# The last batch of attention with its 320-query steps first, in a fused attention and two-product kernel

## The chip, the cores and the metric

One NeuronCore of a Trainium2 chip. The metric is the time of one execution on the device, in microseconds (us). Engines: PE is TensorE (matmuls), PEld its weight loads, DVE VectorE, ACT ScalarE, POOL GpSimd, SP SyncE, which here issues the DMAs.

## The reference

```python
# q, k, v: 4 batches x 8 heads x 576 x 64; s: 4 x 8 x 576
scores = q @ k.T / sqrt(64)                       # per batch and head
cum = cumsum(max(s, 0))
scores = where(causal, -1e9, scores + minimum(-(cum[:, None] - cum[None, :]), 0))
attn = exp(scores - max(scores)); attn /= sum(attn) + 1e-9
x = (attn @ v), heads side by side                # 2304 x 512
h = x @ w_in                                      # 2304 x 2048
x2 = (h * cos(h)) @ w_out                         # 2304 x 512
out = maximum(maximum(x2 @ w1, x2 @ w2), x2 @ w3) @ wo2     # 2304 x 768, then x 512
```

## The kernel before

Nearly every product is made of halves: an operand is split into a high and a low 16-bit part, and three matmuls (high x high, high x low, low x high) stand for one.

**Attention** goes in 32 steps (`STEPS`), a step being one batch b, one query range r and one pair p of heads. Range 0 is queries 0 to 255 (two units of 128 queries), range 1 queries 256 to 575 (units 2, 3, and unit 4 with 64 queries of both heads). A range-0 step sees keys up to 256, a range-1 step all 576. Order before: batch, then range 0, 1, then the four pairs. Steps 20 to 23 are batch 2, range 1; steps 24 to 27 are batch 3, range 0; steps 28 to 31 are batch 3, range 1.

A step does, for each unit: scores on PE (L693, L697), masking and row minimum on DVE (L706), exp on ACT (L712), division and split into halves on ACT (L387) and DVE (L417), and a DMA transpose on SP's queue (L729) into one of two buffers `pt`. Score slots in PSUM, `e` and `pp` have two buffers each. Then the step's values (L759, attention times v) are gathered in one PSUM bank, bank 4, and evacuated as two halves by ACT (L772) and DVE (L777) into `x_b[r][p]`. There is one such buffer for each range and pair, and all batches use it in turn.

**v** of the next batch is loaded (five parts of up to 128 keys), its scale is found, and `v_split` splits each part into a ring of eight buffers. For batches 1 to 3, parts 0 and 1 are split after the last step of the batch before, and parts 2 to 4 ahead of the second step of the batch. Range 0 needs parts 0 and 1, range 1 all five.

**The first product**, h = x w_in, is `mm1(t)`, L906: one block of 16 chunks for each batch and range (`BLOCKS`, t = 2b + r, 0 to 7), each chunk two groups of six matmuls. The first group reads x of pairs 0 and 1, the second of pairs 2 and 3. It is placed behind the last pair of a range, ACT evacuates (L877) from three PSUM banks in turn, and h goes to DRAM.

**The gate and the second product.** Tiles of h come back from DRAM, h cos h is made with ACT's Sin (L1142), which has to wait for the last exp of attention (another table), and L1158 multiplies by w_out. Their scale needs all of w_out converted (L434 to L489, L950, L476). **The last stage** is L1242 and L1205.

**The order of the instructions** is not the program order above. `Plan` collects all operations with an engine, a planned duration, a key, and what they read and write; a write waits for the earlier readers and writers of its bytes. Then it walks through time and gives each engine the ready operation with the lowest key. Attention has keys of about 3 times the step's number, L906 has 1000 and up, L1158 2000 and up, the weight conversions 200 to 600. So attention goes first wherever it is ready, and L906 fills. Each engine then runs its list strictly in that order.

Of the kernel before, what the change touches and what calls it, by code (L numbers as in the profile page):

```python
# [23 lines left out]
B, H, S, D = 4, 8, 576, 64  # L24
# [4 lines left out]
NPAIR = H // 2  # L29
# [6 lines left out]

RANGES = ((0, 256, (0, 1)), (256, 320, (2, 3, 4)))
LAST = 4
STEPS = [(b, r, p) for b in range(B) for r in range(2) for p in range(NPAIR)]
BLOCKS = [(b, r) for b in range(B) for r in range(2)]  # L40
TB = 384
NTB = NT // TB
# [270 lines left out]
def attn_moe_kernel(ctx, tc, qT, kT, v, s, w_in, w_out, w1, w2, w3, wo2, out):  # L313
# [64 lines left out]
    def take(name, ring):  # L378
        n = rings.get(name, 0)
        rings[name] = n + 1  # L380
        return ring[n % len(ring)]
# [63 lines left out]
    def two(buf, cols):  # L445

        return (buf.ap(F16, cols), buf.ap(F16, cols, 2 * cols),
                [buf.span(0, 2 * cols)], [buf.span(2 * cols, 2 * cols)])

    def bound(value, sp, junk, junk_sp, col, col_sp, key, cols=512):  # L450

        P.add("ACT", act(cols, 0.28), key, lambda: nc.scalar.activation(
            out=junk, in_=value, func=AF.Abs, accum_out=col), reads=[sp], writes=junk_sp + [col_sp])

    def weight_load(src, cols, raw, key):
        m = load(raw.ap(I64, cols), src, 1024 * cols, key, writes=[raw.span(0, 8 * cols)])
        P.after(m, [rows_out])
        return raw.ap(I64, cols).bitcast(I32).rearrange("p (n two) -> p n two", two=2)
# [125 lines left out]
    def load_q(st, key):  # L584
        b, r, p = STEPS[st]
        q0, n = ((0, 256), (256, 384))[r]
        hb, lb = take("q", q_ring)
        hs, ls = [hb.span(0, 4 * n)], [lb.span(0, 4 * n)]
        raw = lb.ap(F32, n)
        load(raw, qT[b, p, :, q0:q0 + n], 512 * n, key - LEAD, writes=ls)  # L590
        if b == 0:
            q_of[st] = (raw, None, ls)
            return
        hi, lo = hb.ap(F32R, n), lb.ap(F32R, n)
        scaled(hi, raw, 1.0, key, n, ls, hs, on=Q_ON)
        minus(lo, raw, r_(hi), key + 0.2, n, ls + hs, ls, on=QS_ON)
        q_of[st] = (hi, lo, hs + ls)

    def load_k(b, p, key):
        hb, lb, rb = take("k", k_ring)  # L600
        hs, ls, rs = ([z.span()] for z in (hb, lb, rb))
        raw = lb.ap(F32, S)
        load(raw, kT[b, p], 295e3, key - LEAD, writes=ls, issue=0.65)
        if b == 0 and p == 0:
            row = rb.ap(F32, S)
            for c0, c1 in ((0, 320), (320, S)):
                first_row(c0, c1, row, [rb.span(4 * c0, 4 * (c1 - c0))], -30 if c0 == 0 else F2_KEY)
            ones = one_b.ap(F32, 128)
            bias = [(ones[64 * h:64 * h + 64], row[64 * h:64 * h + 64]) for h in range(2)]
            bias.append((onef_b.ap(F32, 128), row))  # L610
            rs = [rb.span(), one_b.span(), onef_b.span()]
        else:
            row, ones = rb.ap(F32R, S), oner_b.ap(F32R, 128)
            gb = take("got", got_b)
            got, gs = gb.ap(F32, S), [gb.span()]
            for h in range(2):
                load(got[64 * h:64 * h + 2], rows_dram[b * H + 2 * p + h], 4608, key - LEAD,
                     reads=[dspan("rows"), dspan("rows", 1)], writes=gs)
            scaled(row, got, 1.0, key, S, gs, rs, on=K_ON)
            bias = [(ones[64 * h:64 * h + 64], row[64 * h:64 * h + 64]) for h in range(2)]  # L620
            bias.append((onec_b.ap(F32R, 128), row))
            rs = [rb.span(), oner_b.span(), onec_b.span()]
        if b == 0:
            k_of[b, p] = (raw, None, bias, ls + rs)
            return
        hi, lo = hb.ap(F32R, S), lb.ap(F32R, S)
        scaled(hi, raw, 1.0, key, S, ls, hs, on=K_ON)
        minus(lo, raw, r_(hi), key, S, ls + hs, ls, on=KS_ON)
        k_of[b, p] = (hi, lo, bias, hs + ls + rs)
# [9 lines left out]
    def attention(st):  # L639
        b, r, p = STEPS[st]  # L640
        q0, nq, units = RANGES[r]
# [163 lines left out]
    def v_max(b, key):  # L805
        ab, vb = am_b[b % 2], vs_b[b]
        am, vs = ab.ap(F32, 8), vb.ap(F32, 4)
        if b == 0:
            for j in range(5):
                v_load(b, j, key)  # L810
            P.add("DVE", dve1(2560), key, lambda: nc.vector.tensor_reduce(
                out=am[:, 5:6], in_=early_v.ap(F32, 2560), op=ALU.max, axis=AX.X,
                apply_absolute_value=True), reads=[early_v.span()], writes=[ab.span()])
        else:
            for j in range(5):
                t, rb = v_load(b, j, key)
                P.add("DVE", dve1(512), key, lambda j=j, t=t: nc.vector.tensor_reduce(
                    out=am[:, j:j + 1], in_=t, op=ALU.max, axis=AX.X, apply_absolute_value=True),
                    reads=[rb.span()], writes=[ab.span()])
            P.add("DVE", 0.08, key, lambda: nc.vector.tensor_reduce(  # L820
                out=am[:, 5:6], in_=am[:, 0:5], op=ALU.max, axis=AX.X),
                reads=[ab.span()], writes=[ab.span()])
        A = [ab.span()]
        P.add("DVE", dve2(128) + 0.06, key, lambda: nc.vector.tensor_scalar(
            out=dia_b.ap(F32, 128), in0=eye_b.ap(F32, 128), scalar1=am[:, 5:6], scalar2=None,
            op0=ALU.mult), reads=A + [eye_b.span()], writes=[dia_b.span()])
# [36 lines left out]
    def v_split(b, j, key):  # L863
        t, rb = v_load(b, j, key)
        vs = vs_b[b].ap(F32, 4)
        vb = take("v", v_b)
        vv = vb.ap(F16, 1024).rearrange("p (a c) -> p a c", a=2)
        split(vv[:, 0], vv[:, 1], t, vs[:, 1:2], key, 512, [rb.span()], [vs_b[b].span()],
              [vb.span(0, 1024)], [vb.span(1024)], j in V_POOL[b > 0], V_ON)
        v_of[b, j] = (vv, vb)  # L870
# [130 lines left out]
    staged = []  # L1001
    for st in range(len(STEPS)):
        b, r, p = STEPS[st]
        if st + 1 < len(STEPS):
            load_q(st + 1, 3 * st + Q0)
        if r == 0 and p == 1 and b > 0:
            for j in (2, 3, 4):
                v_split(b, j, 3 * st + 1)
        attention(st)
        if r == 1 and b + 1 < B:  # L1010
            load_k(b + 1, p, 3 * st + (6 if p else 3))
            if p == 0:
                v_max(b + 1, 3 * st + 1)
            if p == 1:
                v_scale(b + 1, 3 * st + 1)
            if p == 3:
                for j in range(2):
                    v_split(b + 1, j, 3 * st + 1)
        if st in WI_AT:
            i_ = WI_AT.index(st)  # L1020
            for c in range(NC1 * i_ // len(WI_AT), NC1 * (i_ + 1) // len(WI_AT)):
                rb = take("rw", raw_all)
                key = WI_KEY0 + WI_KEY * c
                words = weight_load(w_in[c], 512, rb, key - 4)
                value, sp = value_of(words, 512, rb.span(), wo_b[c], key)
                small = wg_b[c // G]
                hi, lo, his, los = two(wi_b[c], 512)
                bound(value, sp, hi, his, small.ap(F32, 8)[:, c % G:c % G + 1], small.span(), key)
                staged.append((value, sp, hi, lo, his, los))
                if c % G < G - 1:  # L1030
                    continue
                power(G, small, small, key, POW_BANK)
                h_scale(0, c // G, key)
                by = small.ap(F32, 8)[:, 7:8]
                for i, (value, sp, hi, lo, his, los) in enumerate(staged):
                    split(hi, lo, value, by, key, 512, [sp], [small.span()], his, los,
                          i in WI_POOL, "ACT")
                staged.clear()
        if st == WI_AT[-1]:
            mm1(0)  # L1040
            for g in range(NC1 // G):
                h_scale(1, g, 3 * st + 1)
            out_weights()
        if st == WO_MAX:
            largest_in()
        if p == NPAIR - 1 and st >= NPAIR:
            mm1(2 * b + r)
# [336 lines left out]
```

## Time and profile before

| | |
|---|---|
| median of 3 runs | 868.19 us (866.1 to 868.93) |
| the profiled execution | 869.63 us, span 867.9 us |
| PE busy | 825.9 us, 95% of the span |
| DVE busy | 618.7 us, 71% |
| ACT busy | 536.8 us, 62% |
| mean granted clock of PE | 0.984 |
| DMA, hardware queue | 52.7% of 16 engines' span |

Times inside the span count from its start. Attention ends with the values of step 31 at 366.92 us, the first product at 395.4 us, the second product at 582.5 us; the rest is the last stage. "Busy" is the sum of the durations of an engine's instructions without overlaps. The granted clock is 1.00 at 2.4 GHz and 0.50 at 1.2 GHz.

### The profile page before, as it was taken

What the parts mean: (1) busy time and instruction counts of PE and PEld (TensorE: products, weight loads), DVE (VectorE), ACT (ScalarE), POOL (GpSimd) and SP (SyncE); (2) the same over time, 40 slices, a digit from 0 to 9 for tenths busy, and PEclk for the clock granted to TensorE, in tenths of its full rate; (3) what the DMA queues carried; (4) which work ended last, traced back from release to release, by engine and by line L of the source; (5) the groups of instructions that cost most, each with busy time, mean ns of one, the idle gap of its engine ahead of it and who ended that gap; (6) DMA issues with size and microseconds to landing.
All of it is one profiled execution on the core that took longest, in us unless ns stands there. A gap on an engine that the chain in (4) does not pass through costs nothing.

```text
span 867.9 us, 16606 instructions
## 1 busy us (share of the span) xinstructions
PE 825.9 (95%) x6078; PEld 522.7 (60%) x6078; DVE 618.7 (71%) x1593; ACT 536.8 (62%) x1209; POOL 55.6 (6%) x86
## 2 busy tenths in 40 slices
PE   6887789998999899999999999999999999999998
PEld 3556656786678667878544444446655555555564
DVE  7999998986999789866899999999523213322220
ACT  3778878986887778598999999824112113211211
POOL 4501321111010100000000000000000000000000
PEclk9889989999999989999999999999999999999999
DMA  8789988999999999854354443341000000000001
GB/s 246 172 209 224 263 204 193 242 227 234 245 206 244 222 226 236 223 163 137 108 153 140 135 156 110 112 129 40 1 16 21 13 25 25 1 25 13 37 1 48
DMA packets 156541, 117.70 MB, mean 136 GB/s; under 512 B 109902, under 2 KB 132686, under 8 KB 156460
## 3 DMA queue, kind: packets, MB, share of 16 engines
q1 hardware_dynamic: 156460, 116.65, 52.7%
q8 instruction: 47, 0.77, 0.4%
q14 instruction: 34, 0.28, 0.1%
HBM read 66.67 MB, written 23.74 MB: 104 GB/s over the span
## 4 chain that ended last, share of the span: by engine, by line
PE 64%; DVE 11%; DMA 4%; issue 2%; ACT 1%; POOL 0%; SPq 0%; ACTq 0%; DVEq 0%; POOLq 0%
PE banks L1242 24%; PE banks L1158 22%; PE banks L1205 8%; PE banks L906 7%; DMA p<-p 4%; DVE p L417 3%; DVE p L706 2%; PE banks L759 1%; PE banks L693 1%; DVE p L950 1%; DVE p L437 1%; DVE p L489 1%; ACT p L712 0%; DVE p L440 0%; DVE p L777 0%
## 5 line engine op out<-in xcount | busy, mean ns | idle before, releaser
L1242 PE MATMUL banks<-p,p 128*128 128x384 f16 x1296 | 212.7, 326 | 0.0
L906 PE MATMUL banks<-p,p 128*128 128x256 f16 (+1 forms) x1536 | 203.7, 290 | 1.8 <-ACT p L877 1.8
L1158 PE MATMUL banks<-p,p 128*128 128x512 f16 (+1 forms) x960 | 187.3, 358 | 0.0
L1242 PEld LDWEIGHTS <-p 128*128 128x128 f16 x1296 | 126.6, 98 | 84.8
L906 PEld LDWEIGHTS <-p 128*128 128x128 f16 x1536 | 147.2, 99 | 49.4 <-issue 8.6
L417 DVE SCALAR_TENSOR_TENSOR p<-p,p,p 128x512 f16<-128x512 f32 (+4 forms) x244 | 152.7, 648 | 21.3 <-ACT p L387 20.7
L387 ACT ACTIVATE p<-p,p 128x512 f16<-128x512 f32 (+4 forms) x242 | 144.9, 625 | 33.7 <-DMA p<-p 11.4
L1158 PEld LDWEIGHTS <-p 128*128 128x128 f16 x960 | 93.7, 98 | 91.8
L1257 DVE TENSOR_TENSOR p<-banks,p 128x384 f32<-128x384 f32 x72 | 40.1, 556 | 131.7 <-PE banks L1242 131.7
L877 ACT ACTIVATE p<-banks,p 128x256 f32<-128x256 f32 (+2 forms) x165 | 85.2, 526 | 73.7 <-PE banks L1205 45.4
L486 ACT ACTIVATE p<-p 128x384 f16<-128x384 f32 x36 | 18.8, 522 | 129.5 <-DVE p L1257 119.8
L712 ACT ACTIVATE p<-p,p 128x128 f32<-128x128 f32 (+4 forms) x144 | 82.7, 576 | 15.7 <-DMA p<-in_v_dram 10.9
L1205 PE MATMUL banks<-p,p 128*128 128x512 f16 (+1 forms) x342 | 72.1, 368 | 0.8 <-DVE p L479 0.8
L706 DVE CUSTOM_DVE_ANT_0 p<-banks,p 128x128 f32<-128x128 f32 (+4 forms) x144 | 72.0, 511 | 0.8
L693 PE MATMUL banks<-r,r 64*128 64x256 f32 (+3 forms) x360 | 49.4, 346 | 7.0 <-DVE p L706 6.2
L1205 PEld LDWEIGHTS <-p 128*128 128x128 f16 x342 | 33.5, 98 | 36.3 <-issue 1.0
L1147 DVE SCALAR_TENSOR_TENSOR p<-p,p 128x512 f32<-128x512 f32 (+1 forms) x80 | 50.0, 632 | 5.5 <-ACT p L1145 5.4
L486 ACT ACTIVATE p<-p,p 128x512 f16<-128x512 f32 (+1 forms) x64 | 40.0, 672 | 19.9 <-DVE p L481 15.2
L759 PE MATMUL banks<-p,p 128*64 128x64 f16 (+2 forms) x1056 | 41.5, 231 | 10.3 <-DMA p<-p 9.5
L1139 DVE SCALAR_TENSOR_TENSOR p<-p,p 128x512 f32<-128x512 int32 (+1 forms) x80 | 49.3, 632 | 1.5 <-ACT p L1137 0.9
L759 PEld LDWEIGHTS <-p 128*64 128x64 f16 x1056 | 36.5, 111 | 21.7 <-issue 13.5
L1145 ACT ACTIVATE p<-p 128x512 f32<-128x512 f32 (+1 forms) x80 | 45.4, 577 | 0.1
(95 smaller groups left out, 787.5 us busy)
## 6 DMA issues: line engine op xcount, KB each, us to landing
p<-h_dram SPq DMA_DIRECT2D x64, 256.0 KB
p<-in_moe_w_out_dram SPq DMA_DIRECT2D x22, 512.0 KB
h_dram<-p SPq DMA_DIRECT2D x32, 320.0 KB
p<-in_moe_w_dram SPq DMA_DIRECT2D x18, 512.0 KB
p<-in_moe_w_in_dram SPq DMA_DIRECT2D x16, 512.0 KB
h_dram<-p SPq DMA_DIRECT2D x32, 256.0 KB
p<-in_v_dram SPq DMA_DIRECT2D x28, 256.0 KB
p<-in_k_dram SPq DMA_DIRECT2D x16, 288.0 KB
```

The costliest lines, as they stand in the source:

```text
L387: "ACT": (slow(cols, 0.19 if par else 0.09), lambda: nc.scalar.activation(out=out, in_=src, func=AF.Copy, scale=by)),
L417: n = P.add("DVEP", dve1(cols) + 0.06, key, lambda: nc.vector.scalar_tensor_tensor(out=lo, in0=src, scalar=by, in1=hi, op0=ALU.mult, op1=A ...
L486: P.add("ACT", slow(cols), key, lambda: nc.scalar.activation(out=hi, in_=src_, func=AF.Copy, scale=by), reads=reads, writes=hi_sp)
L693: nc.tensor.matmul(sp[:, o:o + kn], qq[rows_of[h], at:at + 128], kk[rows_of[h], k0:k0 + kn], start=(m == 0 and bool(opens)), stop=False)
L706: nc.vector.tensor_tensor_reduce(out=e, in0=sc, in1=km, op0=ALU.add, op1=ALU.min, scale=-0.125, scalar=3.0e38, accum_out=mn[:, j:j + 1]),
L712: "ACT", act(n, 0.28), tg, lambda j=j, e=e, mn=mn, sm=sm: nc.scalar.activation(out=e, in_=e, func=AF.Exp, scale=-1.0, bias=mn[:, j:j + 1], ...
L759: nc.tensor.matmul(to, vv[:, vp, (2 * p + h) * 64:(2 * p + h + 1) * 64], moving, start=(j == 0 and z == 0 and part == 0), stop=(j == nj - ...
L877: "ACT": (act(cols, 0.05 if by is None else 0.15), lambda: nc.scalar.activation(out=out, in_=src, func=AF.Copy, scale=1.0 if by is None el ...
L906: nc.tensor.matmul(hp, w[:, wp, ks], xx, start=(k == 0 and m == 0), stop=(k == KD - 1 and m == 2),)
L1158: nc.tensor.matmul(bank(base + d)[:, 0:n], w[:, wp, ds], xx, start=(c == 0 and z == 0), stop=(c == NC1 - 1 and z == 2))
L1205: nc.tensor.matmul(o, hv[:, hp, 128 * i:128 * i + 128], wv[:, wp, c0:c1], start=(f == 0 and m == 0), stop=(f == NC2 - 1 and m == 2))
L1242: nc.tensor.matmul(bank(base + m)[:, 0:TB], w[:, wp, ks], xx, start=(k == 0 and z == 0), stop=(k == KD - 1 and z == 2))
```

## The change

In the last batch the ranges change places: steps 24 to 27 are now range 1, steps 28 to 31 range 0. The calls of `mm1` follow: block 7 is multiplied before block 6. Since range 1 needs all five parts of v, all five are split after the last step of batch 2. Nothing else is edited; the plan, the rings and the DMA order follow from the new program.

```diff
-STEPS = [(b, r, p) for b in range(B) for r in range(2) for p in range(NPAIR)]
+STEPS = [(b, r, p) for b in range(B) for r in ((1, 0) if b == B - 1 else (0, 1)) for p in range(NPAIR)]
...
-        if r == 0 and p == 1 and b > 0:
+        if r == 0 and p == 1 and 0 < b < B - 1:
             for j in (2, 3, 4):
                 v_split(b, j, 3 * st + 1)
         attention(st)
...
             if p == 3:
-                for j in range(2):
+                for j in range(5 if b + 1 == B - 1 else 2):
                     v_split(b + 1, j, 3 * st + 1)
```

## Rows read from the trace of the kernel before

**Rows 1.** The page, engines: busy us (share of the span), instructions

```profile
PE 825.9 (95%) x6078; PEld 522.7 (60%) x6078; DVE 618.7 (71%) x1593; ACT 536.8 (62%) x1209; POOL 55.6 (6%) x86
```

**Rows 2.** Windows, PE: stretch, length, busy (instructions), granted clock, DMA share, GB/s

```profile
100.00:105.00 5.00, 1.60 (x13) 1.00 1.14 304
105.00:110.00 5.00, 4.05 (x26) 0.67 0.83 237
...
200.00:205.00 5.00, 2.78 (x28) 1.00 0.71 159
...
264.00:293.00 29.00, 27.01 (x340) 1.00 1.08 241
...
300.00:305.00 5.00, 2.79 (x17) 0.97 1.08 223
305.00:311.40 6.40, 6.24 (x32) 0.50 0.88 247
...
341.60:366.90 25.30, 24.36 (x298) 1.00 0.99 244
366.90:395.40 28.50, 28.50 (x253) 1.00 0.54 168
```

**Rows 3.** Waits of PE, 264 to 395.4: total us, times, longest

```profile
PE banks L759 <- DMA p<-p: 2.8, 3, 1.8
PE banks L476 <- DVE p L473: 0.9, 1, 0.9
```

**Rows 4.** Timeline, PE: start, length, first shape of the merged group [idle before]

```profile
202.93 0.35 PE L693 MATMUL banks<-r,r 64*128 64x256 f32 x1 [2.05 <-DVE p L706]
...
264.12 0.98 PE L693 MATMUL banks<-r,r 64*128 64x256 f32 x12
...
290.68 0.69 PE L759 MATMUL banks<-p,p 128*64 128x256 f16 x12 [0.37 <-DVE p L777]
...
293.61 2.62 PE L906 MATMUL banks<-p,p 128*128 128x320 f16 x18
...
305.16 1.17 PE L759 MATMUL banks<-p,p 128*64 128x256 f16 x12 [1.78 <-DMA p<-p]
...
327.21 1.81 PE L759 MATMUL banks<-p,p 128*64 128x256 f16 x54
...
343.67 1.81 PE L759 MATMUL banks<-p,p 128*64 128x256 f16 x54
...
353.82 8.69 PE L906 MATMUL banks<-p,p 128*128 128x256 f16 x78
...
368.67 26.91 PE L906 MATMUL banks<-p,p 128*128 128x256 f16 x198
395.42 23.71 PE L1158 MATMUL banks<-p,p 128*128 128x256 f16 x204
```

**Rows 5.** Timeline, ACT: a split of v, step 28's evacuation, the first Sin

```profile
287.14 0.72 ACT L387 ACTIVATE p<-p,p 128x512 f16<-128x512 f32 x1 [1.11 <-PE banks L759]
...
339.50 0.43 ACT L772 ACTIVATE p<-banks 128x320 f16<-128x320 f32 x1
...
371.81 0.72 ACT L1142 ACTIVATE p<-p 128x256 f32<-128x256 f32 x2
```

**Rows 6.** Timeline, DVE: the second half of two evacuations (steps 23 and 28)

```profile
290.13 0.49 DVE L777 SCALAR_TENSOR_TENSOR p<-banks,p 128x320 f16<-128x320 f32 x1 [1.49 <-ACT p L772]
...
341.03 0.48 DVE L777 SCALAR_TENSOR_TENSOR p<-banks,p 128x320 f16<-128x320 f32 x1
```

**Rows 7.** Chain that ended last: issue and length of three transposes up to their landing

```profile
274.14 7.52 DMA p<-p
...
285.08 4.08 DMA p<-p
...
300.19 4.92 DMA p<-p
```

**Rows 8.** Timeline, SP's queue: one issue

```profile
300.19 1.24 SPq L729 DMA_TRANSPOSE p<-p  x1
```

## The prediction

> **What bounds the kernel now.** I read the page first: TensorE is busy for 95% of the span [rows 1]. So I asked where it is not, and which of those places the change can touch. The two orders can differ only from the scores of step 24 on, which start at 264.12 us [rows 4]; the views from there to 395.4 us, where the last block of the first product (L906) ends, are the ones that count. In the windows of TensorE [rows 2] the reader is to see that it loses 1.99 us in 264 to 293, 2.21 us in 300 to 305, 0.16 us in 305 to 311.4 and 0.94 us in 341.6 to 366.9: 5.3 us in 131. On top of that it runs at a granted clock of 0.50 (1.2 GHz) for the 6.4 us from 305, which is 3.2 us of lost work. So 8.5 us is all that a better order could win here. The list of waits [rows 3] names the two largest causes: 2.8 us for transposes that values (L759) need, and 0.9 us for the power of the gate's scale. From 366.9 us on TensorE is full at a clock of 1.00, and the timeline [rows 4] shows the gate's product starting at 395.42 right behind the last L906. The first Sin runs at 371.81 [rows 5], 23.6 us ahead of that. So what decides is TensorE's idle time and clock between 264 and 395 us, and not how early attention ends: TensorE has a block or more of L906 in hand whenever attention is late.
>
> **What the change does to that filler.** x_b has one buffer for each pair and each range, x_b[0][p] and x_b[1][p]. The evacuation of a step's values (L772, L777) writes it, and the block of L906 made of the four pairs reads it, up to its last chunk. Before, the ranges alternate, so a step writes the buffer of the block before the last one. I number L906's blocks by batch and range, 0 to 7. The rows show this wait already: the values of step 28 (batch 3, 320 queries, pair 0) run at 327.21 [rows 4], but their evacuation at 339.50 [rows 5], when block 5 has got to its last chunk; the values of step 29 follow at 343.67. These 10.5 us cost TensorE nothing, since block 6 was ready and fills it.
>
> In the new order steps 20 to 23 and steps 24 to 27 are both of the 320-query range. Step 24's result must go into x_b[1][0], which block 5 still has to read, and block 5 can only start when step 23 is evacuated and block 4 is done. That is at 293.61 us, as before [rows 4], because scores and values go ahead of L906 in either order. Bank 4 holds one step's values, so step 25's values wait for step 24's evacuation, and step 27's transposes wait for step 25's values (pt has two buffers). Attention therefore stands from step 24's values, about 292 us, until block 5 has been multiplied: 192 matmuls of 136 ns (26.91 us for 198, [rows 4]) are 26.1 us, with the scores of the waiting steps between them. I call the end of block 5's last reader T; it comes at some 330 us. Until T TensorE has work. After T it has none in hand: block 4 is gone, and a chunk of block 7 (the next in order) needs all four pairs of steps 24 to 27.
>
> **The hole behind T, step by step.** An evacuation takes from 339.50 to 341.51, 2.0 us, in one row pair [rows 5, 6], with L777 queued on VectorE behind another instruction; I take 1.7. Values take 1.81 us [rows 4]. So step 24's evacuation ends at T+1.7 and step 25's values at T+3.5. Only then can step 27's three transposes go. An issue holds SP for 1.24 us and more [rows 8], so the third goes out at T+6.5 or so, and a transpose lands 4.08, 4.92 or 7.52 us after its issue [rows 7]; I take 4.9, since the weight loads that share the queue stay. Step 27's values start at T+11.4 and end at T+13.2, and its evacuation at T+14.9. From there block 7 runs freely. If the transposes cost nothing, the chain through bank 4 alone (four evacuations, three values) would take 12.2 us; at 7.52 us it takes 17.5.
>
> TensorE's own work in that time: block 5's last half chunk, 0.8; values of steps 25, 26, 27, 5.4; first halves of three chunks of block 7 (pairs 0 and 1 only, three banks), 2.5. Together 8.7 us. So idle time is 3.5 to 8.8 us, and I take 6.2. Scores of the 256-query steps to come (0.98 us and more a step, [rows 4]) have two slots in PSUM and go ahead of block 5; those of two steps that are late enough to fall in here would take 2.0 us off the lower end, which is 1.5.
>
> **The clock.** In the one place where the trace of this stretch has a like hole, 2.79 us busy in 300 to 305, the clock falls to 0.50 for the 6.4 us behind it [rows 2]. A stretch at 100 to 105, 1.60 us busy, is followed by 0.67. But at 200 to 205, also only 2.78 us busy, it stays at 1.00. The hole behind T is longer than each of these, and ahead of step 27's values (T+7.0 to T+11.4, less the half chunks) it has a wait of 2 to 4 us in one piece, so I take the fall, 3.2 us, and keep 0 as the lower bound. The Trainium skill ("TensorE: Matmul & The Clock Gate", section "Part 1: The HAM clock gate") says that the throttled state is the default and that activity releases it; by that rule a hole like this one is always paid twice, and the sum would be 873.0 us. By the row at 200 it is paid once, and the sum would be 869.8.
>
> **The other parts, each at nothing.** *V parts 2 to 4 one step earlier than step 25:* same loads and splits; two of the buffers are freed by step 23's values, and the split that waited for them already ran at 287.14, released by L759 [rows 5]. Step 24's values come at 291 or later, when bank 4 is free (L759 at 290.68 waits for L777, [rows 4]), and that covers the split. Without this cover it is a few tenths of a us. *Transposes and loads of q on SP's queue:* a step of 320 queries transposes 38 blocks of 128 columns and one of 256 has 12; the sums are equal, 26 blocks a step only change places. More of them fall before 293 us, where TensorE already loses 1.99 us; there L906 of block 4 covers them, and I keep 1.99. *The last block* is now block 6, 192 matmuls of 111 ns (8.69 us for 78, [rows 4]) or 21.4 us instead of 26.1: the same work in another order. It covers the Sin table and the first gate chunk, which today start 23.6 us early. *VectorE* has the same work in all; while attention stands it converts weights, which it would do anyway.
>
> **The sum.** Idle and lost work after: 1.99 (264 to 293) + 1.0 (waits for scores and transposes between 293 and T, or under block 7; bounds 0 and the 2.4 of today) + 6.2 (hole) + 0.94 (gate's scale) + 3.2 (clock) = 13.3 us, against 8.5 today. That is +4.8 us. The profiled execution took 869.63 us, 1.4 above the median of 868.19 of the runs shown; its own sum is 874.4, and against the median it is 873.0.
>
> **Rivals.**
> *Hole without the fall of the clock:* 10.1 against 8.5, +1.6 us, 869.8: no change that shows. For it speaks the row at 200 to 205; against it that the other two did fall and that this hole is longer.
> *Faster:* between 293 us and T, TensorE has a whole uninterrupted block 5, so the waits of 300 to 305 and the fall behind them go (5.6 us gained with the 0.16). If the transposes land at once, because attention's own are absent, and the scores of two steps fall into the hole, it is 1.5 us without a fall: 2.0 + 0 + 1.5 + 0.9 = 4.4 against 8.5, 864.1. It decides below 5.9 us in all, that is a hole under 3 us. For it: the queue is less loaded while attention stands. Against it: without those scores the chain through bank 4 alone leaves 3.5 us.
> *A longer stop:* the evacuation of step 24 stands in ScalarE's order and the transposes of step 27 in SP's, and what is ordered behind them stands too: L877 of block 5's last chunks, stores of h, loads of q for the 256-query steps. If these come late by one transpose's latency more (7.5 us instead of 4.9) and once more for step 28's, the hole has 5 us more: 878. For it: the order is set by planned times, and today's 2.05 us at 202.93 and 1.78 at 305.16 [rows 4] are such misses. Against it: at 339.50 the evacuation waited without any idle time on ScalarE ahead of it.
> *The change changes nothing:* if block 5 ended before step 24's values, there would be no stop. It can't start before step 23 is evacuated, L777 at 290.13 [rows 6], and takes 26 us, so I give it nothing of its own.
>
> **How the numbers follow.** Under 0.3% (2.6 us) a measurement of this kernel can't tell from no change. Hole and fall 0.45 (873, own range 870 to 876; 0.05 of it below 870.8), longer stop 0.15 (876 to 882), hole without fall 0.25 (867.5 to 871; 0.03 on the faster side, 0.02 on the slower), faster 0.15 (863 to 866; 0.03 of it within 0.3%). So slower 0.57, same 0.28, faster 0.15. The range of 8 in 10 runs from 866, the short hole, to 879, the longer stop.
>
> **What would show it.** In the profile after: L772 of the first 320-query step of batch 3 waits some 35 us after its values; L906 runs almost unbroken from 293 to about 330 us; then some 15 us in which TensorE is busy for 8 to 10, waiting for transposes and for L777; a granted clock near 0.5 behind it; the first L1158 at about 400 us instead of 395.4, and everything from there shifted by as much. I am wrong if TensorE has L906 work in that stretch (the buffer was free), if the idle time sits elsewhere, or if the part behind L1158's start changes its length.

## The result, and the profile after

The changed kernel takes 876.47 us (median of 4, 873.62 to 879.03) against 867.63 us of the kernel before: a ratio of 1.0113, 95% interval 1.0082 to 1.0145. It is slower, by 8.8 us. The forecast was 873.0, in a range of 866 to 879. A second measurement of the same kernel, on another occasion, gave 878.26 against 865.86, 1.0134 (1.0107 to 1.0162). The ratios are formed over the executions and are not the quotients of the two medians; two of the 25 executions of the kernel before beside e1 to e4, at 1058.56 and 1692.43 us, are left out of them (without these two its median of 865.28 us is 864.75).

The profiled execution took 879.03 us, with a span of 877.3. First the page of the changed kernel, engines (compare [rows 1]):

```profile
PE 829.2 (95%) x6078; PEld 525.0 (60%) x6078; DVE 619.3 (71%) x1595; ACT 537.7 (61%) x1209; POOL 54.3 (6%) x84
```

The busy times of PE, DVE and ACT are those of before to within half a per cent, and PE's number of instructions is the same. The mean granted clock is 0.977, against 0.984. So the span grew by waiting and by the clock, and not by work. Windows as in [rows 2], cut where the changed kernel's stages end: stretch, length, busy time of PE, PEld, DVE, ACT and POOL, granted clock, DMA share, GB/s.

```profile
264.00:293.00 29.00, 28.17 (x317) 23.24 (x315) 26.20 (x77) 24.62 (x60) 2.90 (x4) 1.00 1.07 235
293.00:330.00 37.00, 36.51 (x328) 26.73 (x326) 34.73 (x105) 29.56 (x71) 0.92 (x2) 1.00 1.00 248
330.00:353.40 23.40, 12.92 (x212) 10.69 (x210) 17.57 (x62) 10.51 (x32) 0.00 (x0) 0.85 0.59 114
353.40:372.30 18.90, 16.46 (x136) 11.49 (x134) 9.55 (x44) 11.61 (x33) 0.00 (x0) 1.00 0.74 190
372.30:404.50 32.20, 32.14 (x270) 26.52 (x271) 17.79 (x46) 26.49 (x73) 0.00 (x0) 0.95 0.60 192
404.50:877.30 472.80, 468.70 (x2613) 254.85 (x2611) 275.54 (x550) 231.62 (x427) 0.00 (x0) 1.00 0.20 64
```

The reader is to see one hole: TensorE is nearly full up to 330 us (1.3 us idle), then idle for 10.5 of 23.4 us, and the granted clock falls in it. The last stretch, from the first L1158 on, is 472.8 us long; in the kernel before, 395.4 to the span's end is 472.5. All of the difference but 0.3 us lies ahead of it.

The timeline of TensorE in the changed kernel, from step 24's values to the first L1158 (compare [rows 4]), and below it ACT's first half of the evacuations of steps 24 and 27 (compare [rows 5]):

```profile
293.03 1.83 PE L759 MATMUL banks<-p,p 128*64 128x256 f16 x54
294.79 3.43 PE L906 MATMUL banks<-p,p 128*128 128x320 f16 x24
...
327.65 2.62 PE L906 MATMUL banks<-p,p 128*128 128x320 f16 x18
331.55 1.81 PE L759 MATMUL banks<-p,p 128*64 128x256 f16 x54 [1.27 <-DVE p L777]
335.46 1.81 PE L759 MATMUL banks<-p,p 128*64 128x256 f16 x54 [2.10 <-DVE p L777]
337.21 2.62 PE L906 MATMUL banks<-p,p 128*128 128x320 f16 x18
345.59 0.58 PE L693 MATMUL banks<-r,r 64*128 64x256 f32 x1 [5.76 <-DVE p L706]
...
348.46 3.25 PE L759 MATMUL banks<-p,p 128*64 128x256 f16 x54
352.77 0.69 PE L759 MATMUL banks<-p,p 128*64 128x256 f16 x12 [1.05 <-DVE p L777]
353.39 1.80 PE L906 MATMUL banks<-p,p 128*128 128x320 f16 x12
...
372.36 1.11 PE L759 MATMUL banks<-p,p 128*64 128x256 f16 x12 [2.31 <-DMA p<-h_dram]
373.40 31.29 PE L906 MATMUL banks<-p,p 128*128 128x320 f16 x258
404.53 15.66 PE L1158 MATMUL banks<-p,p 128*128 128x256 f16 x142
```

```profile
330.55 0.42 ACT L772 ACTIVATE p<-banks 128x320 f16<-128x320 f32 x1
...
351.75 0.44 ACT L772 ACTIVATE p<-banks 128x320 f16<-128x320 f32 x1 [2.37 <-PE banks L759]
```

Step 24's values end at 294.8 and their evacuation runs at 330.55: 35.7 us of standing attention, against 10.5 us for step 28 before. From the end of block 5, 330.3, to 353.39, when block 7 runs on, it is 23.1 us. In them TensorE has the values of steps 25, 26 and 27, 18 matmuls of block 7 (the three half chunks) and a few scores. Nothing else is in hand, as block 5 is done and block 7 lacks the last two pairs.

Two lists hold up step 27 in this hole. The first is SP's: three issues of transposes, and the DMA share behind them.

```profile
335.57 2.85 SPq L729 DMA_TRANSPOSE p<-p  x1
339.52 1.20 SPq L729 DMA_TRANSPOSE p<-p  x1
340.77 1.40 SPq L729 DMA_TRANSPOSE p<-p  x1
```

```profile
344.00:346.00 2.00, 0.41 (x1) 0.79 0.00 0
```

The first and the third of these are step 27's second and last; the one between them is step 28's first, and it has to wait for step 28's split (L417 on 128 x 128, a shape that only the 256-query steps have; it ends at 339.45). Step 27's last one is issued at 340.77, and from 344 to 346 no DMA runs. The second list is VectorE's, in the chain that ended last:

```profile
342.64 0.59 DVE p L950
...
344.32 0.55 DVE p L417 x2
...
345.11 0.43 DVE p L706 x2
```

Step 31's scores, which stand ahead of step 27's values on TensorE, wait for this L706. It stands behind a split (L417) whose first half ScalarE had done at 341.4, and that one stands behind VectorE's work for the gate's scale (maxima over w_in, L950, and their powers, L464 to L473).

The clock, from windows of TensorE alone in the same kernel:

```profile
345.60:351.90 6.30, 5.83 (x70) 0.50 0.27 46
...
372.30:376.20 3.90, 3.84 (x24) 0.56 0.25 77
```

It stands at half for 6.3 us out of the hole, and once more behind the wait of 2.31 us ahead of the last step's values, which the profile puts down to a load of h.

**The account.** Idle time from 264 to 404.5: 0.83 + 0.49 + 10.48 + 2.44 + 0.06 = 14.3 us; lost to the lower clock: 5.83 x 0.50 + 3.84 x 0.44 = 4.6 us. Together 18.9, against 8.5 before: 10.4 us. To free the comparison from what happens earlier, which differs by a us or two from one execution to the next, I measure from the values of step 21, which are the same work in all these kernels, to the first L1158. Before, that is 259.21 to 395.42, 136.2 us; after, 257.75 to 404.53, 146.8 us. The difference is 10.6 us. I use this stretch below as well; its name is "the stretch". In the profile of the second measurement (e5) it is 145.6 us, 9.4 more than before; where the rest of that measurement's 12.4 us between the medians lies isn't shown.

### The profile page after: what moved, and what is told of

Read it like the earlier page. It is cut to its first block, busy times and chain, and to the rows that moved or that the text cites. A ratio compares the mean times of both kernels' runs of the same rounds, so it can differ in the third digit from the quotient of the medians.

```text
span 877.3 us, 16589 instructions
## 1 busy us (share of the span) xinstructions
PE 829.2 (95%) x6078; PEld 525.0 (60%) x6078; DVE 619.3 (71%) x1595; ACT 537.7 (61%) x1209; POOL 54.3 (6%) x84
## 4 chain that ended last, share of the span: by engine, by line
PE 48%; DVE 27%; ACT 10%; DMA 9%; issue 4%; POOL 1%; SPq 1%; DVEq 0%; ACTq 0%; POOLq 0%
PE banks L1242 22%; PE banks L906 11%; PE banks L1205 8%; DVE p L417 6%; DMA p<-p 4%; ACT p L387 3%; DVE p L706 3%; PE banks L693 3%; PE banks L759 2%; DVE p L437 2%; DVE p L1139 2%; DVE p L1147 2%; DVE p L440 2%; ACT p L1142 2%; ACT p L1145 2%
## 5 line engine op out<-in xcount | busy, mean ns | idle before, releaser
L1158 PE MATMUL banks<-p,p 128*128 128x512 f16 (+1 forms) x960 | 187.3, 358 | 0.0
L417 DVE SCALAR_TENSOR_TENSOR p<-p,p,p 128x512 f16<-128x512 f32 (+4 forms) x244 | 152.9, 649 | 24.4 <-ACT p L387 23.8
L387 ACT ACTIVATE p<-p,p 128x512 f16<-128x512 f32 (+4 forms) x241 | 144.2, 624 | 27.4 <-DVE p L720 5.3
L1158 PEld LDWEIGHTS <-p 128*128 128x128 f16 x960 | 93.6, 98 | 91.8
L706 DVE CUSTOM_DVE_ANT_0 p<-banks,p 128x128 f32<-128x128 f32 (+4 forms) x144 | 71.8, 510 | 0.8
L693 PEld LDWEIGHTS banks<-r,r 64*128 64x128 f32 (+1 forms) x360 | 33.9, 197 | 24.2 <-DVE p L706 11.3
```

The source lines that it names most:

```text
L387: "ACT": (slow(cols, 0.19 if par else 0.09), lambda: nc.scalar.activation(out=out, in_=src, func=AF.Copy, scale=by)),
L417: n = P.add("DVEP", dve1(cols) + 0.06, key, lambda: nc.vector.scalar_tensor_tensor(out=lo, in0=src, scalar=by, in1=hi, op0=ALU.mult, op1=A ...
L693: nc.tensor.matmul(sp[:, o:o + kn], qq[rows_of[h], at:at + 128], kk[rows_of[h], k0:k0 + kn], start=(m == 0 and bool(opens)), stop=False)
L706: nc.vector.tensor_tensor_reduce(out=e, in0=sc, in1=km, op0=ALU.add, op1=ALU.min, scale=-0.125, scalar=3.0e38, accum_out=mn[:, j:j + 1]),
L1158: nc.tensor.matmul(bank(base + d)[:, 0:n], w[:, wp, ds], xx, start=(c == 0 and z == 0), stop=(c == NC1 - 1 and z == 2))
```

## The experiments

Four kernels were timed beside one another, then four more. "Before" and "changed" are the two kernels of this case.

**e1: buffers of their own.** The changed kernel, but steps 24 to 27 write x into four new buffers, laid over a part of k's ring that is free by then.

```diff
+x_last = Buf(nc, att0 + 6912, 5120).ring(NPAIR)
...
-        xb = x_b[r][p]
+        xb = x_last[p] if b == B - 1 and r == 1 else x_b[r][p]
```

> The changed kernel, but the four 320-query steps of batch 3 write x into buffers of their own (x_last, laid over the ring entry of k that the last pair of batch 2 leaves free) instead of x_b[1]. One-buffer theory: step 24's L772 follows its values within 5 us, no hole of TensorE behind block 5, no half clock there: 863 to 869 us, at least 8 us under the changed kernel's 876.5. Rival, tail: the small steps at the end cost time by themselves (the wait of 2.3 us for the last values at 372 us and the half clock behind it), so it stays at 872 or more. Rival, split: the early split of five parts of v costs, so it stays near 876.

Measured: 867.30 us against 865.28, 1.0038 (1.0016 to 1.0059). The stretch is 136.8 us. The timeline of its TensorE:

```profile
296.17 1.81 PE L759 MATMUL banks<-p,p 128*64 128x256 f16 x54
...
307.01 1.81 PE L759 MATMUL banks<-p,p 128*64 128x256 f16 x54
...
323.30 1.81 PE L759 MATMUL banks<-p,p 128*64 128x256 f16 x54
331.72 1.89 PE L759 MATMUL banks<-p,p 128*64 128x256 f16 x54
337.91 0.69 PE L759 MATMUL banks<-p,p 128*64 128x256 f16 x12 [2.24 <-DMA p<-p]
...
392.32 23.71 PE L1158 MATMUL banks<-p,p 128*128 128x256 f16 x204
```

Here step 24's values (296.17) are followed by its evacuation at 299.60, 1.6 us after they end, and the next steps come in 8 to 16 us each beside block 5. There is no hole behind block 5 (the longest wait is of 2.24 us) and no half clock from 264 to 392 us. The order of the ranges is that of the changed kernel, and so is the early split of v. So the one buffer makes most of the loss, and the rivals "tail" and "split" fall as its main cause. About 0.4% over the kernel before is left in the medians; its stretch shows only 0.5 us of it, and what it is stays open.

**e2: the same buffers in the old order,** where steps 28 to 31 use them.

```diff
-        xb = x_b[r][p]
+        xb = x_last[p] if b == B - 1 and r == 1 else x_b[r][p]
```

> The kernel before, with the same buffers of their own for the 320-query steps of batch 3 (steps 28 to 31), order unchanged. One-buffer theory as the prediction has it: the 10.5 us that step 28's evacuation waits cost TensorE nothing, since block 6 fills them, so within 0.3% of the kernel before (865 to 870). Rival: a waiting attention always costs, whatever the filler: 860 to 864.

Measured: 866.28 against 865.28, 1.0020 (1.0004 to 1.0037). Taking away step 28's 10.5 us of waiting wins nothing. The wait alone is free while TensorE has another block in hand; that is the difference between the same wait before and after the change.

**e3: the split alone.** Old order, all five parts of v split behind step 23.

```diff
-        if r == 0 and p == 1 and b > 0:
+        if r == 0 and p == 1 and 0 < b < B - 1:
...
-                for j in range(2):
+                for j in range(5 if b + 1 == B - 1 else 2):
```

> The kernel before in its old order, but all five parts of v of batch 3 are split after step 23. One-buffer theory: the same as before within 0.3% (865 to 870). Rival, split: 870 or more, part of the 8.8 us.

Measured: 864.45 against 865.28, 0.9996 (0.9969 to 1.0024). This half of the change costs nothing.

**e4: one scores call moved.** In the changed kernel the scores of step 31 stand ahead of step 27's values in TensorE's list (the 5.76 us at 345.59). Here they are put behind them.

```diff
+                n_score = P.add("PE", ..., scores, ...)
+                P.after(n_score, [values_of[27]] if st == 31 else [])
```

> The changed kernel, but the scores of step 31 are ordered behind the values of step 27, which they precede on TensorE in the changed kernel (5.8 us of waiting for L706 in the hole). If the hole is set by bank 4 and the transposes, as the prediction priced it (12 to 17.5 us), and the rest of its 23 us by this order, the hole shrinks by 3 to 6 us and the time is 870 to 874. Rival: the transposes of step 27 land no earlier than these scores start, then the wait only changes its name and the time stays at 875 to 878.

Measured: 873.23 against 865.28, 1.0097 (1.0059 to 1.0134), beside the changed kernel's 1.0113 and 1.0134. The time lies where the first theory put it, but the intervals overlap, so as a gain it isn't shown. The timeline of its TensorE, and below it pieces of its chain that ended last, tell what stood behind the scores:

```profile
328.48 1.81 PE L759 MATMUL banks<-p,p 128*64 128x256 f16 x54 [1.27 <-DVE p L777]
...
336.80 0.30 PE L759 MATMUL banks<-p,p 128*64 128x256 f16 x2 [0.23 <-DVE p L706]
340.94 2.94 PE L759 MATMUL banks<-p,p 128*64 128x64 f16 x52 [3.85 <-DMA p<-p]
...
347.50 1.17 PE L759 MATMUL banks<-p,p 128*64 128x256 f16 x12 [2.46 <-DVE p L777]
348.60 1.78 PE L906 MATMUL banks<-p,p 128*128 128x320 f16 x6
```

```profile
335.59 0.62 DVE p L417 x2
...
336.26 1.19 SPq L729
...
337.50 3.41 DMA p<-p
...
340.94 1.05 PE banks L759 x12
341.99 3.58 DMA p<-p
...
345.68 0.52 ACT p L387
...
347.05 0.41 DVE p L777
```

Step 25's values end at 330.3 and step 27's last transpose is there at 340.9, 10.6 us later, where I had reckoned 7.9. The chain says why: this transpose is issued at 337.50, behind one of step 28 (336.26), which waited for step 28's split (L417, 335.59). Step 27's values run on 13.7 us behind block 5's end, against 18.2 in the changed kernel. But behind them ScalarE's list stands too: the evacuation (L772, at 346.49) comes after a split (L387, 345.68) that waits for the next transpose of step 28, and TensorE waits 2.46 us for its second half, L777. So most of the wait has passed to other lists. From the end of block 5 at 327.2 to the restart of block 7 it is 21.4 us instead of 23.1.

**e5: the changed kernel again,** as the partner of the next three.

> The changed kernel once more, beside the runs that follow and the kernel before on the same chip. All theories: 1.008 to 1.015 of the kernel before.

Measured: 878.26 against 865.86, 1.0134 (1.0107 to 1.0162). The stretch is 145.6 us (258.42 to 403.99), and the hole is the same: 5.77 us for L706 at 346.64. The second fall of the clock is missing here; at its place the wait is a little shorter, and the clock stays at 1.00:

```profile
372.96 0.69 PE L759 MATMUL banks<-p,p 128*64 128x256 f16 x12 [1.93 <-DMA p<-h_dram]
```

**e6: buffers of their own for two pairs of four,** steps 24 and 25 only.

```diff
-        xb = x_b[r][p]
+        xb = x_last[p] if b == B - 1 and r == 1 and p < 2 else x_b[r][p]
```

> The changed kernel, but only the first two of the four 320-query steps of batch 3 (24 and 25) write x into buffers of their own; 26 and 27 still write x_b[1][2] and x_b[1][3]. One-buffer theory, chain through bank 4 and pt: step 27's transposes go ahead of the end of block 5, so behind it stand only two evacuations and one or two values, a hole of 5 to 7 us in place of 23 and no half clock or a short one: 866 to 870. Rival: any wait for block 5 costs the whole stop: 873 to 878.

Measured: 866.42 against 865.86, 1.0007 (0.9983 to 1.0031). Step 26 still waits: its values end at 325.2 and its evacuation runs at 335.51. Behind that stand only one more values call and its evacuation, as its TensorE shows:

```profile
323.43 1.81 PE L759 MATMUL banks<-p,p 128*64 128x256 f16 x54
...
337.43 1.81 PE L759 MATMUL banks<-p,p 128*64 128x256 f16 x54
341.33 0.69 PE L759 MATMUL banks<-p,p 128*64 128x256 f16 x12 [2.09 <-DVE p L777]
```

The granted clock is 1.00 in every 5 us from 320 to 380 here. So what counts is not that attention waits for block 5, but how many serial steps are left behind T: with two evacuations and a values call it costs nothing that shows, with four, three and the transposes in between it costs 9 to 12 us.

**e7: the hole filled.** The changed kernel with 48 matmuls on constants, 8 behind step 25's values and 40 behind step 26's; nothing reads their result.

```diff
+        for q in (0, 0) + (1,) * 10 if st == 27 else ():
+            P.add("PE", 0.65, 999, lambda: busy(4), reads=[..., x_of[7, q][2].span()], writes=[bspan(7)])
         if p == NPAIR - 1 and st >= NPAIR: mm1(2 * b + r)
```

> The changed kernel with 48 matmuls of 384 columns on constants added to TensorE, 8 behind step 25's place and 40 behind step 26's values; their result is not used. They take 7.8 us of the hole at full clock. If the fall of the clock behind the hole costs what the prediction says (3 us), and the fillers stand where TensorE waits anyway, the granted clock stays at 1.00 between 330 and 355 us and the time falls to 871 to 875. Rival, only the wait counts: the clock stays up but the time does not change (875 to 878); if the fillers push values back, 878 or more.

Measured: 874.23 against 865.86, 1.0083 (1.0055 to 1.0110), where the changed kernel beside it has 1.0134 (1.0107 to 1.0162): 4.0 us less with more work. Five of its six executions lie below all six of the changed kernel. Windows of TensorE, two in e7 and then the first of them in the changed kernel (e5):

```profile
330.00:355.00 25.00, 22.10 (x290) 1.00 0.71 130
264.00:399.80 135.80, 128.73 (x1292) 1.00 0.85 207
```

```profile
330.00:355.00 25.00, 14.64 (x226) 0.86 0.57 107
```

The clock never leaves 1.00 in e7. In the stretch e7 is 2.5 us shorter than e5 (143.1 against 145.6), so the half clock's part in the loss, with what follows from it, is some 2.5 to 4 us. The hole itself stays: step 27's values come at 347.19, 16.0 us behind step 25's at 331.23, where the changed kernel has 16.9 (348.46 and 331.55). From the end of block 5 to the restart of block 7 it is 20.7 us, against 23.1 (22.7 in e5).

**e8: the cause put into the old order.** The kernel before; steps 24 to 27 (256 queries) write x into x_b[1], where block 5 still reads, and steps 28 to 31 into buffers of their own.

```diff
-        xb = x_b[r][p]
+        xb = x_b[r][p] if b < B - 1 else x_last[p] if r == 1 else x_b[1][p].sub(0, 1024)
```

> The kernel before in its old order, but steps 24 to 27 (256 queries) write x into x_b[1], where block 5 still reads, and steps 28 to 31 into buffers of their own. One-buffer theory: the old order now has the stop too, step 24's evacuation waits for the end of block 5 and TensorE has no block in hand behind it; transposes and values of a 256-query step are shorter, so a hole of 10 to 18 us: 871 to 880. Rival, order: what costs is the order of the ranges, so this stays within 0.3% of the kernel before (863 to 870).

Measured: 882.68 against 865.86, 1.0181 (1.0140 to 1.0222): 16.8 us slower than the kernel before, in that kernel's own order, and no faster than the changed kernel (878.26). The rival "order" falls. Windows of its TensorE:

```profile
320.00:336.00 16.00, 8.81 (x88) 1.00 0.48 124
...
371.00:384.90 13.90, 3.91 (x77) 0.67 0.51 111
```

There are two holes. The first, 7.2 us idle, is the one forecast. The second, 10.0 us idle of 13.9, wasn't: the last 320-query step comes so late that block 6 is used up as well, and its values wait 7.1 us, by the profile for a load of h, and 2.9 us for transposes. It is why 882.7 lies above the 871 to 880 expected. The changed kernel has no such second hole; that its small steps at the end spare it is argued. A wait in the first hole, from the timeline:

```profile
325.40 0.69 PE L759 MATMUL banks<-p,p 128*64 128x256 f16 x12 [2.62 <-DVE p L777]
```

In all of this first hole the clock stays at 1.00.

## Why the prediction was right

*What bounds the stretch* was right: only TensorE's idle time and clock ahead of L1158 count; behind it the two kernels differ by 0.3 us.

*The buffer as the cause* was right, and is shown from three sides: taken away (e1, e6) the loss goes, put into the old order (e8) it comes (its first hole, 7.2 us idle), and where TensorE has another block in hand (before, beside e2) the same wait is free.

*Where T is and what TensorE has until then:* block 5 unbroken to 330 us, as forecast. The waits of 300 to 305 and the half clock behind them are gone; idle time there is 0.5 us where I had allowed 1.0, and 0.8 up to 293 us where I had kept 1.99.

*The hole* is the term that was sized too small. I take the prediction's T here, the last half chunk ahead of block 5's end, 329.5: 14.9 us forecast, 23.9 measured; idle 6.2 forecast, 10.5 measured. Step 25's values end 3.9 us behind T (3.5 forecast): 0.4 us more. From there to the landing of step 27's last transpose it is 10.8 us (340.77 plus the 3.41 us that it takes in e4), and not 7.9: 2.9 us more. Then step 27's values start only at 348.46, as step 31's scores stand ahead of them, wait until 345.59 and run at half clock: 4.3 us more. The values take 3.25 us instead of 1.81, for the same reason: 1.4 us more. Evacuation and restart are as reckoned. Together 9.0 us.

Both large parts are of the kind that the rival of the longer stop described: what is ordered behind a waiting instruction waits too. Its price was 5 us, and its place a queue of ScalarE or SP. SP's queue it was for the transposes: one issue held SP for 2.85 us, and step 28's transpose stood ahead of step 27's last. The last transpose itself took less than assumed, 3.41 us (in e4) for 4.9. The other place was TensorE's own list, with VectorE's behind it; VectorE's work on the weights, priced at nothing, stands in the chain of the hole. By e4 these lists hide one another, and ScalarE's with them: with the scores out of the way the hole was 1.7 us shorter and not 4.3.

*The clock:* one fall of 3.2 us was forecast; the one behind the hole cost 2.9. The Trainium skill ("TensorE: Matmul & The Clock Gate", section "Part 1: The HAM clock gate (the "warmup" mystery)") says that activity releases the throttle. The trace of e7 agrees: where the hole is filled, the clock stays at 1.00. That a hole is always paid twice, as the prediction went on, isn't borne out: the first hole of e8 leaves 7.2 of 16 us idle at a clock of 1.00. The second fall, 1.7 us behind a wait of 2.31 us at 372, and this wait itself, were not foreseen. SP's queue holds step 31's last transpose at 365.79 between loads of h (365.08 and 368.58). In the chain this transpose takes 3.96 us, and a load of h, 2.50 us from 369.81, ends the wait; that the plan set these loads for an earlier end of attention is argued and was not tried.

*The sum:* 13.3 forecast and 18.9 measured in the profiled execution, against 8.5. The gate's 0.94 us is gone, which I had kept. Between the medians it is +8.8 us for a forecast of +4.8, past the likeliest case (870 to 876) and at the lower end of the longer stop (876 to 882). In the second measurement it is +12.4 us, which from 868.19 would be 880.6, above the range. So the mechanism was right and the size too small by nearly half; the time lies in the range by its upper end, which the longer stop had set. Of the parts priced at nothing the split was so (e3), and the last block, with 0.06 us idle. The order of the transposes on SP's queue and VectorE's work on the weights were not, in the hole.

## What to carry to other kernels

Before work is reordered, list the buffers that alternate by the order, and see which one is written twice in a row: its writer will wait for the last reader of the block between. Such a wait is free as long as the bound engine has another finished block to work on, and is paid, here with a fall of the clock on top, when the waiting work is what the next block is made of. The size is then the serial chain behind the release (evacuation, bank, transposes, values), with whatever stands ahead of its parts in each engine's list, and cutting that chain in half, as two spare buffers of four did here, can be worth as much as removing the wait.

## What the runs showed of the hardware

Matmuls that nobody needs made the kernel 4.0 us faster between the medians (e7). They stood where TensorE waits in the changed kernel and its granted clock falls; with them it stayed at 1.00. The waits that lowered the clock in the changed kernel were of 5.76 us (345.59) and of 2.31 us (372.36); others of 1.27 and 2.10 us (331.55, 335.46) left it at 1.00. But the length of one wait doesn't tell it: in e8 a wait of 2.62 us (325.40) left the clock at 1.00, and in e1 one of 2.24 us (337.91) did.

The three transposes of a step took 10.6 us from their release to the last landing (e4, 330.3 to 340.9), but that is not the time of three transposes: one issue held SP for 2.83 us, and a transpose of the next step, which was not ready, stood between the second and the third. The third itself took 3.41 us from its issue to its landing.
